# Older value rows copied on the chip by GpSimd instead of loaded, and small constants loaded from ScalarE's queue

## The chip, the cores and the metric

The kernel runs on one core of a Trainium2 chip. The metric is the device time of one execution in microseconds, as a median of runs. Engines are named as in the profile: PE (TensorE, matmuls; PEld its weight loads), DVE (VectorE), ACT (ScalarE), POOL (GpSimd), SP (SyncE, which here only issues DMAs). A DMA can be issued from the queue of any engine that has one; here nearly all are issued by SP, some indirect ones by POOL.

## The reference: what is computed

Attention with a local window and a few global keys, then a mixture of experts with one expert per token.

```python
# attention: B=4, H=8, S=768, D=64, n_global=8, n_local=96
scores = scale * q @ k.T - slope[h] * dist
keep = (key < n_global) | ((0 <= row - key) & (row - key < n_local))
a = softmax(where(keep, scores, -1e9)) ; attn = a @ v
# experts: x = attn as (3072, 512), E=8, F=1024
logits = x @ w_gate + modality_bias[modality_id]
e = argmax(logits) ; g = softmax(logits)[e]
out = g * (relu(x @ w1[e]) @ w2[e])
```

All is fp32. So a block of 128 queries needs the values of its own 128 tokens, of the 96 tokens ahead of it, and of the first 8 tokens of its batch.

## The kernel before

**Blocks and steps.** The 3072 tokens are 24 blocks of 128 (6 per batch). `step(n)`, n from 0 to 24, writes out by hand what PE, ACT and DVE do, in order (a manual schedule): scores of block n (`s_mm`, L257), their reduction and exponential (`red`: DVE L276, ACT L287), the values' product of block n-2 (`pv`), transposes of the probabilities of block n-1 (`t_mm` on PE L301, `t_cp` on DVE L310), normalisation and store of block n-2 (`xr`, L355 and L362), parts of the gate of blocks n-3 and n-4, transposes of the queries and keys of block n+1 (`k_mm` L215, `k_cp` with ACT L228 and DVE L224, L233), the copies of values `copyv(n-1)` on POOL, and whatever is due in that step (`todo`: constants, routing, planning, the first expert's weights). The order on SP and POOL is not by hand: a scheduler sets it, from a list of what each instruction waits for.

**Values.** Scores of a block are two halves of 64 queries, and `pv` multiplies, for each half, a 40-row part (L322) and a 128-row part (L334). There are four kinds of tiles. `va[r]` (four of them) holds a block's 128 value rows for all heads, loaded by SP (L122, 256 KB). `vo` (three) is the 128-row operand of the first half: 64 rows of this block (POOL copy L135) and the upper 64 rows of the block before (POOL copy L137). `vl[r]` (four) is the 40-row operand: for each half, in partitions 0 to 31 for even heads and 64 to 95 for odd ones, 32 older value rows, and in partitions 32 to 39 and 96 to 103 the 8 global rows, which POOL copies from `vg` (L142) when a buffer is first used in a batch. The 32 older rows are rows 32 to 63 of the block before for the first half and rows 64 to 95 for the second. `loadv` loads them from HBM with four DMAs of 32 KB for every block that isn't the first of its batch. `loadv(1)` is called twice, once ahead of the steps (L1048) and again in step 0, so block 1's values are loaded twice.

**Queues.** A DMA counts on one of eight completion semaphores in turn, and its issue waits for the landing of the one eight places before it. SP issues queries, keys and values two to three steps ahead, then stores, zeros for the list of sorted tokens (`consts_c`, L1029, from `zrow`) and weights. `consts_l` (L974 to L981: the gate's weights `wg`, the modality ids `mi`, the modality bias `mb`, the two sizes `gi`) is due in step 1 and is issued by SP. ACT starts with the table load that belongs to L228.

**Routing.** When a batch of blocks has been gated, `route_a` and `route_b` work out every token's position in its expert's list; for the first three batches POOL does this (L427 to L433: `base`, `pos`). `route_d` on DVE takes them up (L442, L444), and `route_c` on POOL scatters the token numbers, two scatters of 128 tokens a step (L450). The copies on POOL that come after such a pair in its order carry waits for its landing. Steps 18 to 20 scatter the second batch; then SP loads the first units' token lists (`uie`), POOL gathers their rows (`xge`, L628), and the third batch's positions follow. After step 24 the experts begin: the first layer of the units in `eslots`, then the rest.

Of the kernel before, what the change touches and what calls it, by code (L numbers as in the profile page):

```python
# [12 lines left out]
I32 = mybir.dt.int32  # L13
# [6 lines left out]
P = 128  # L20
B, H, S, D = 4, 8, 768, 64
NP = H // 2
DM = H * D
E = 8
FF = 1024
NT = B * S
NBLK = NT // P
# [40 lines left out]
def moe_attention_kernel(ctx, tc, q, k, v, n_global, n_local, modality, w_gate, mod_bias, w1, w2, out):  # L68
    nc = tc.nc
# [39 lines left out]
    NV = 4  # L109
    va = [a1.tile([P, H, D], F32, name=f"va{i}") for i in range(NV)]  # L110
    vo = [a1.tile([P, H, D], F32, name=f"vo{i}") for i in range(3)]
    vl = [a1.tile([P, 2, NP, D], F32, name=f"vl{i}") for i in range(NV)]
# [4 lines left out]
    def loadv(n):  # L117
        b, i = n // NB, n % NB
        r, a = n % NV, P * i

        def rows(dst, r0, cnt, hs):
            nc.sync.dma_start(dst, v[b, hs, r0 : r0 + cnt, :].rearrange("h s d -> s h d"))  # L122

        rows(va[r], a, P, slice(0, H))
        if i == 0:
            for h in range(2):
                rows(vg[b % 2][64 * h + 32 : 64 * h + C1], 0, NG0, slice(h, H, 2))
        else:
            for x in range(2):
                for h in range(2):  # L130
                    rows(vl[r][64 * h : 64 * h + 32, x], a - 96 + 64 * x, 32, slice(h, H, 2))

    def copyv(n):
        b, i, r = n // NB, n % NB, n % NV
        nc.gpsimd.tensor_copy(vo[n % 3][0:64], va[r][0:64])  # L135
        if i:
            nc.gpsimd.tensor_copy(vo[n % 3][64:P], va[(n - 1) % NV][64:P])  # L137
        if vb[r] != b:
            vb[r] = b
            for h in range(2):  # L140
                g = slice(64 * h + 32, 64 * h + C1)
                nc.gpsimd.tensor_copy(vl[r][g], vg[b % 2][g].unsqueeze(1).broadcast_to([NG0, 2, NP, D]))  # L142

    load_kq(0)
    load_kq(1)
    loadv(0)


# [534 lines left out]
    def l1_unit(s, f):  # L683
        if f % 2 == 0:
            s.ph = p_t(f"ph{s.name}{f}")
        fs = slice(f * P, (f + 1) * P)
        o = s.ph[:, f % 2 * U : (f % 2 + 1) * U]
        for c in range(4):
            hi, lo = s.hi["a", c], s.lo["a", c]
            nc.tensor.matmul(o, hi[:, fs], s.xh[:, c, :], start=(c == 0), stop=False)  # L690
            nc.tensor.matmul(o, hi[:, fs], s.xl[:, c, :], start=False, stop=False)  # L691
            nc.tensor.matmul(o, lo[:, fs], s.xh[:, c, :], start=False, stop=(c == 3))  # L692
        if f % 2:
            fsl = slice(f - 1, f + 1)
            pv = s.ph.rearrange("p (f n) -> p f n", f=2)
            nc.scalar.activation(s.hh[:, fsl, :], pv, AF.Relu)  # L696
            V.scalar_tensor_tensor(s.hl[:, fsl, :], pv, 0.0, s.hh[:, fsl, :].bitcast(F32), ALU.max, ALU.subtract)  # L697
# [227 lines left out]
    def at(n, f, *args):  # L925
        todo.setdefault(n, []).append((f, args))
# [5 lines left out]
    wg = const.tile([P, 4, 32], F32, name="wg")  # L932
# [38 lines left out]
    mod = {}  # L971

    def consts_l():
        nc.sync.dma_start(wg[:, :, 0:E], w_gate.rearrange("(c p) e -> p c e", p=P))  # L974
        mi = gp.tile([NBLK, P, 2], I32, tag="mi", name="mi", bufs=1)
        nc.sync.dma_start(mi, modality.bitcast(I32).rearrange("(t p w) -> t p w", t=NBLK, w=2))
        mb = gp.tile([P, 2, E], F32, tag="mb", name="mb", bufs=1)
        nc.sync.dma_start(mb, mod_bias.rearrange("(o m) e -> o m e", o=1).broadcast_to([P, 2, E]))
        gi = gp.tile([P, 2, 2], I32, tag="gi", name="gi", bufs=1)
        for j, src in enumerate((n_global, n_local)):  # L980
            nc.sync.dma_start(  # L981
                gi[:, j, :], src.bitcast(I32).rearrange("(o w) -> o w", o=1).broadcast_to([P, 2])
            )
        mod["mi"], mod["mb"], mod["gi"] = mi, mb, gi
# [47 lines left out]
    for b in range(B):  # L1032
# [4 lines left out]
        for j in range(NB):  # L1037
            at(n0 + NB + (6 + j // 2 if b + 1 < B else 5), route_c, b, j)
    at(1, consts_a)
    at(1, consts_l)  # L1040
    at(3, consts_b)
    for j in range(8):
        at(3 + j, consts_c, j)
    at(4, consts_d)
    for h in range(H):
        table(tbl, h, mm)
    load_kq(2)
    loadv(1)  # L1048

    early = {}  # L1050
# [46 lines left out]
    def l1_first(f):  # L1097
        l1_unit(eslots[0], f)

    man_pe = tc.manual_schedule(engines={ET.PE})  # L1100
    man_pe.__enter__()
    man = tc.manual_schedule(engines={ET.Activation, ET.DVE})
# [2 lines left out]
    def load(n):  # L1105

        if n + 3 < NBLK:
            load_kq(n + 3)
        if n + LV < NBLK:
            loadv(n + LV)  # L1110
# [10 lines left out]
    def step(n):  # L1121
# [36 lines left out]
        if back:  # L1158
            t_mm(n - 1, 3)
            t_cp(n - 1, 3, not on)  # L1160
            copyv(n - 1)
# [103 lines left out]
    for u in range(nslot):  # L1265
# [3 lines left out]
        for m in range(0 if u else LF, 16):  # L1269
            if m >= 8:  # L1270
                for t in range(s.halves):
                    if u + 1 < nslot or s.halves == 1:
                        l2(s, m - 8, t)
                    else:
                        p = 2 * (m - 8) + t
# [102 lines left out]
```

## Time and profile before

| | us |
|---|---|
| median of 3 runs | 502.28 (501.94 to 502.31) |
| the profiled execution's own time | 504.03 |
| its span in the trace | 502.2 |
| granted TensorE clock, mean | 0.987 |
| attention, to about | 190 |
| experts, from about | 190 |

The trace is of the profiled execution, so its durations belong to 504.03 us, not to the median. In its rows a start time is followed by the busy time, the engine, the line, the operation, what it writes and reads, and in brackets how long the engine had waited and for whom. SPq is SP's queue, with the time that the issue of a DMA took. In rows of stretches stand the busy time of PE, PEld, DVE, ACT and POOL, then the granted clock, the busy share of the DMA engines and the GB/s that they moved.

### The profile page before, as it was taken

The numbers are of one execution on the slowest core, as the hardware profiler recorded it, in microseconds if no ns is written. First come the engines' busy times: TensorE is split into PE (matmuls) and PEld (weight loads), VectorE is DVE, ScalarE is ACT, GpSimd is POOL, SyncE is SP. The second block draws the span as 40 slices with busy tenths as digits, with TensorE's granted clock in tenths as the row PEclk, the third lists the DMA queues.
The fourth block names the chain that finished last, engine by engine and source line by source line (L and its number), as shares of the span: only waits on it lengthen the run. The fifth ranks groups of instructions, "written<-read, shape, count | busy, mean of one in ns | idle before, by whom it ended". The sixth has DMA issues, their size and how long they took to land.

```text
span 502.2 us, 15068 instructions
## 1 busy us (share of the span) xinstructions
PE 468.6 (93%) x5789; PEld 419.4 (84%) x5789; DVE 343.1 (68%) x999; ACT 297.5 (59%) x716; POOL 156.3 (31%) x234
## 2 busy tenths in 40 slices
PE   7879899999898989999999999899999999999991
PEld 6778899999787869898989898798988998798980
DVE  5868788978987874997756477474765748556530
ACT  6747777777667763546456466464665557555420
POOL 9513314545443355062130405204041040500100
PEclk9989999999989999999999999999999999999997
DMA  9778878787668934767785849778598666965100
GB/s 175 152 215 206 200 168 215 180 196 192 158 160 248 287 128 150 265 188 246 232 277 199 275 154 325 246 220 292 159 332 269 205 248 218 321 225 165 44 22 26
DMA packets 125509, 102.75 MB, mean 205 GB/s; under 512 B 96283, under 2 KB 97715, under 8 KB 125428
## 3 DMA queue, kind: packets, MB, share of 16 engines
q1 hardware_dynamic: 120660, 88.65, 60.8%
q0 software_dynamic: 4768, 13.05, 7.2%
q8 instruction: 47, 0.77, 0.6%
q14 instruction: 34, 0.28, 0.2%
HBM read 87.31 MB, written 14.63 MB: 203 GB/s over the span
## 4 chain that ended last, share of the span: by engine, by line
PE 44%; issue 12%; DVE 2%; DMA 2%; POOL 1%; ACT 0%; SPq 0%; POOLq 0%; DVEq 0%; ACTq 0%
PE phs L692 5%; PE phs L690 4%; PE phs L691 4%; PE pos L730 4%; PE pos L729 4%; PE pos L728 4%; PE phe L690 2%; PE phe L691 2%; PE phe L692 2%; PE poe L728 2%; PE poe L730 2%; PE poe L729 2%; DMA uig<-ids_sorted 2%; POOL out L744 1%; PE mts L673 1%
## 5 line engine op out<-in xcount | busy, mean ns | idle before, releaser
L287 ACT ACTIVATE pr<-sc,nmx 128x168 f32<-128x168 f32 x192 | 81.1, 423 | 30.5 <-DVE nmx L276 29.4
L692 PE MATMUL phs<-xhs,als 128*128 128x256 f32 x256 | 72.5, 283 | 0.6 <-DVE als L662 0.5
L690 PE MATMUL phs<-xhs,ahs 128*128 128x256 f32 x256 | 72.2, 282 | 0.0
L691 PE MATMUL phs<-xls,ahs 128*128 128x256 f32 x256 | 72.1, 282 | 0.0
L628 POOL DMA_INDIRECT xgs<-x_rows,uis x16 | 27.1, 1694 | 131.5 <-DMA uis<-ids_sorted 66.9
L276 DVE CUSTOM_DVE_ANT_0 sc<-s,tbl 128x168 f32<-128x168 f32 x192 | 52.1, 327 | 9.4 <-PE s L257 9.4
L697 DVE SCALAR_TENSOR_TENSOR hls<-phs,hhs 128x512 fp32r<-128x512 f32 x32 | 22.1, 692 | 51.0 <-ACT hhs L696 51.0
L301 PE MATMUL pt<-ident,pr 128*128 128x128 f32 x288 | 47.2, 288 | 7.3 <-DVE pT L310 4.7
L728 PE MATMUL pos<-bhs,hhs 128*128 128x512 f32 x128 | 51.4, 401 | 0.0
L730 PE MATMUL pos<-bhs,hls 128*128 128x512 f32 x128 | 50.6, 395 | 0.0
L729 PE MATMUL pos<-bls,hhs 128*128 128x512 f32 x128 | 50.5, 395 | 0.0
L692 PEld LDWEIGHTS phs<-xhs,als 128*128 128x128 f32 x256 | 48.8, 191 | 1.0 <-DVE als L662 1.0
L310 DVE COPY pT<-pt 128x384 f32<-128x384 f32 x71 | 38.9, 548 | 15.5 <-PE pt L301 15.4
L690 PEld LDWEIGHTS phs<-xhs,ahs 128*128 128x128 f32 x256 | 48.9, 191 | 0.4
L691 PEld LDWEIGHTS phs<-xls,ahs 128*128 128x128 f32 x256 | 48.8, 191 | 0.3
L696 ACT ACTIVATE hhs<-phs 128x512 fp32r<-128x512 f32 x32 | 19.1, 597 | 50.0 <-PE phs L692 50.0
L257 PEld LDWEIGHTS s<-kt,qt 64*64 64x64 f32 x1536 | 38.2, 132 | 10.4 <-ACT kt L228 6.1
L257 PE MATMUL s<-kt,qt 64*64 64x128 f32 (+1 forms) x1536 | 41.7, 248 | 4.7 <-ACT kt L228 1.8
L301 PEld LDWEIGHTS pt<-ident,pr 128*128 128x128 f32 x288 | 32.4, 144 | 13.1 <-DVE pT L310 5.4
L450 POOL DMA_INDIRECT ids_sorted<-tki,pi x24 | 25.4, 1060 | 34.7 <-DVE remb L508 17.6
L287 ACT ACTIVATION_READ_ACCUMULATOR pr<-sc,nmx 128x1 f32 x192 | 35.9, 187 | 0.0
L744 POOL DMA_INDIRECT out<-obs,ois x16 | 17.1, 1069 | 47.7 <-ACT obs L743 44.6
(343 smaller groups left out, 1251.2 us busy)
## 6 DMA issues: line engine op xcount, KB each, us to landing
va<-in_v SPq DMA_DIRECT2D x25, 256.0 KB, 4.2
kn<-in_k SPq DMA_DIRECT2D x24, 256.0 KB, 4.0
qn<-in_q SPq DMA_DIRECT2D x24, 256.0 KB, 5.0
x_rows<-xr SPq DMA_DIRECT2D x24, 256.0 KB, 3.7
vl<-in_v SPq DMA_DIRECT2D x84, 32.0 KB, 3.0
rawe0a<-in_moe_w SPq DMA_DIRECT2D x4, 512.0 KB, 5.9
rawe0b<-in_moe_w SPq DMA_DIRECT2D x4, 512.0 KB
rawe1a<-in_moe_w SPq DMA_DIRECT2D x4, 512.0 KB, 3.5
```

Source lines behind the costliest of these rows:

```text
L257: nc.tensor.matmul(ps[h][64 * half : 64 * half + 64, c : c + cnt], qt[hs, hp, 64 * half : 64 * half + 64], keys, start=True, stop=True,)
L276: V.tensor_tensor_reduce(out=sc, in0=pss[n, hp // 2][h][:, hp % 2 * W : (hp % 2 + 1) * W], in1=(tbl0 if n % NB == 0 else tbl)[:, hh, :], o ...
L287: last[0] = nc.scalar.activation(pr[:, h * (PRW - W) : h * (PRW - W) + W], sc, AF.Exp, bias=nmx[:, hh : hh + 1], scale=-1.0, accum_out=sum ...
L301: nc.tensor.transpose(tp[:, j * P : (j + 1) * P], pr[:, o : o + P], ident)
L310: V.tensor_copy(pT.rearrange("p a b -> p (a b)"), tp[:, 0 : 3 * P])
L628: nc.gpsimd.indirect_dma_start(out=s.xg[:, t, :], out_offset=None, in_=s.xsrc, in_offset=bass.IndirectOffsetOnAxis(ap=s.ui[:, t, 0:1], axi ...
L690: nc.tensor.matmul(o, hi[:, fs], s.xh[:, c, :], start=(c == 0), stop=False)
L691: nc.tensor.matmul(o, hi[:, fs], s.xl[:, c, :], start=False, stop=False)
L692: nc.tensor.matmul(o, lo[:, fs], s.xh[:, c, :], start=False, stop=(c == 3))
L728: nc.tensor.matmul(s.po[t], s.hh[:, fc, tt], hi[:, wv], start=(fc == 0), stop=False)
L729: nc.tensor.matmul(s.po[t], s.hh[:, fc, tt], lo[:, wv], start=False, stop=False)
L730: nc.tensor.matmul(s.po[t], s.hl[:, fc, tt], hi[:, wv], start=False, stop=(fc == 7))
```

## The change

Two things. `loadv` no longer loads the older 32 rows; `copyv` copies them on POOL from the `va` tile of the block before, four copies of 32 partitions x 256 columns for each block with a predecessor (new L138), each to other partitions than it reads from. That is 80 copies for 84 DMAs of 32 KB. And `consts_l` issues its five DMAs from ACT's queue, and is called ahead of the manual schedules instead of in step 1. What PE and DVE do, and in which order, is unchanged. Lines of the changed kernel are shifted: L135, L137 and L142 become L131, L134 and L143, and later ones are one higher.

```diff
--- before.py
+++ after.py
@@ -125,16 +125,17 @@
         if i == 0:
             for h in range(2):
                 rows(vg[b % 2][64 * h + 32 : 64 * h + C1], 0, NG0, slice(h, H, 2))
-        else:
-            for x in range(2):
-                for h in range(2):
-                    rows(vl[r][64 * h : 64 * h + 32, x], a - 96 + 64 * x, 32, slice(h, H, 2))
 
     def copyv(n):
         b, i, r = n // NB, n % NB, n % NV
         nc.gpsimd.tensor_copy(vo[n % 3][0:64], va[r][0:64])
         if i:
-            nc.gpsimd.tensor_copy(vo[n % 3][64:P], va[(n - 1) % NV][64:P])
+            back = va[(n - 1) % NV]
+            nc.gpsimd.tensor_copy(vo[n % 3][64:P], back[64:P])
+
+            for x in range(2):
+                for h in range(2):
+                    nc.gpsimd.tensor_copy(vl[r][64 * h : 64 * h + 32, x], back[64 * x + 32 : 64 * x + 64, h:H:2])
         if vb[r] != b:
             vb[r] = b
             for h in range(2):
@@ -971,14 +972,14 @@
     mod = {}
 
     def consts_l():
-        nc.sync.dma_start(wg[:, :, 0:E], w_gate.rearrange("(c p) e -> p c e", p=P))
+        nc.scalar.dma_start(wg[:, :, 0:E], w_gate.rearrange("(c p) e -> p c e", p=P))
         mi = gp.tile([NBLK, P, 2], I32, tag="mi", name="mi", bufs=1)
-        nc.sync.dma_start(mi, modality.bitcast(I32).rearrange("(t p w) -> t p w", t=NBLK, w=2))
+        nc.scalar.dma_start(mi, modality.bitcast(I32).rearrange("(t p w) -> t p w", t=NBLK, w=2))
         mb = gp.tile([P, 2, E], F32, tag="mb", name="mb", bufs=1)
-        nc.sync.dma_start(mb, mod_bias.rearrange("(o m) e -> o m e", o=1).broadcast_to([P, 2, E]))
+        nc.scalar.dma_start(mb, mod_bias.rearrange("(o m) e -> o m e", o=1).broadcast_to([P, 2, E]))
         gi = gp.tile([P, 2, 2], I32, tag="gi", name="gi", bufs=1)
         for j, src in enumerate((n_global, n_local)):
-            nc.sync.dma_start(
+            nc.scalar.dma_start(
                 gi[:, j, :], src.bitcast(I32).rearrange("(o w) -> o w", o=1).broadcast_to([P, 2])
             )
         mod["mi"], mod["mb"], mod["gi"] = mi, mb, gi
@@ -1037,7 +1038,6 @@
         for j in range(NB):
             at(n0 + NB + (6 + j // 2 if b + 1 < B else 5), route_c, b, j)
     at(1, consts_a)
-    at(1, consts_l)
     at(3, consts_b)
     for j in range(8):
         at(3 + j, consts_c, j)
@@ -1097,6 +1097,7 @@
     def l1_first(f):
         l1_unit(eslots[0], f)
 
+    consts_l()
     man_pe = tc.manual_schedule(engines={ET.PE})
     man_pe.__enter__()
     man = tc.manual_schedule(engines={ET.Activation, ET.DVE})
```

SP's order in the fill, before, from block 3's keys to the second load of block 1's values (`kn`, `qn`: keys and queries; `va_76` to `va_79` are the four `va`, `vl_83` to `vl_86` the four `vl`):

```order
L105 DMA kn_274<-in_k 128x8x64
L105 DMA qn_275<-in_q 128x8x64
L122 DMA va_78<-in_v 128x8x64
L122 DMA vl_85<-in_v 32x4x64 x4
L974 DMA wg<-in_moe_w_gate 128x4x8
L105 DMA kn_358<-in_k 128x8x64
L105 DMA qn_359<-in_q 128x8x64
L976 DMA mi<-in_moe_modality_id 24x256
L978 DMA mb<-in_moe_modality_bias 128x16
L981 DMA gi<-in_n_global 128x2
L122 DMA va_77<-in_v 128x8x64
L122 DMA vl_84<-in_v 32x4x64 x4
```

and the same stretch now (`ids_sorted<-zrow` are the zeros of `consts_c`):

```order
L105 DMA kn_278<-in_k 128x8x64
L105 DMA qn_279<-in_q 128x8x64
L122 DMA va_78<-in_v 128x8x64
L122 DMA va_79<-in_v 128x8x64
L1030 DMA ids_sorted<-zrow 128x388 x2
L122 DMA vg_88<-in_v 8x4x64 x2
L105 DMA kn_358<-in_k 128x8x64
L105 DMA qn_359<-in_q 128x8x64
L1030 DMA ids_sorted<-zrow 128x388 x4
L122 DMA va_77<-in_v 128x8x64
L1030 DMA ids_sorted<-zrow 128x388 x2
```

The loads of `vl` and of the constants are gone from it, and block 3's values and six writes of zeros have moved ahead of the second load of `va_77`.

On ACT the five constants now stand ahead of its first table load (L228, now L229): `mi`, `mb`, `gi` twice, then `wg`, which waits for an earlier DMA's landing and for POOL's memset of `wg` (L970). All else on ACT keeps its order.

POOL's order from the second scatter of step 20 to the third batch's positions (`base`), before (waits on DMASW are for the landing of scatters and gathers):

```order
L450 DMA ids_sorted<-tki,pi_3287 24832x16
L628 DMA xge_4275<-x_rows,uie_4064 128x512 [waits DMAHW4_49,DMAHW3_49,DMAHW7_49,DMAHW1_49,DVE_49]
L628 DMA xge_4275<-x_rows,uie_4064 128x512
L628 DMA xge_4278<-x_rows,uie_4075 128x512 [waits DMAHW5_49]
L628 DMA xge_4278<-x_rows,uie_4075 128x512
L135 COPY vo_81<-va_78 64x512 [waits DMAHW1_49,PE_49]
L137 COPY vo_81<-va_77 64x512 [waits DMASW5_49,DMASW6_49,DMASW4_49,DMASW7_49,DMASW3_49,DMASW2_49]
L135 COPY vo_82<-va_79 64x512 [waits DMAHW5_49,PE_49]
L137 COPY vo_82<-va_78 64x512
L427 TENSOR_TENSOR base<-base,pks_4262 128x8 [waits DVE_49,Pool_49]
```

and now:

```order
L451 DMA ids_sorted<-tki,pi_3279 24832x16
L138 COPY vl_86<-va_78 32x256 [waits DMASW3_49,DMAHW2_49,DMASW2_49,PE_49]
L138 COPY vl_86<-va_78 32x256 [waits PE_49] x3
L131 COPY vo_81<-va_78 64x512 [waits PE_49,Pool_49]
L134 COPY vo_81<-va_77 64x512 [waits Pool_49]
L629 DMA xge_4263<-x_rows,uie_4052 128x512 [waits DMAHW3_49,DMAHW4_49,DMAHW1_49,DMAHW7_49,DVE_49,Pool_49]
L629 DMA xge_4263<-x_rows,uie_4052 128x512
L629 DMA xge_4266<-x_rows,uie_4063 128x512 [waits DMAHW5_49]
L629 DMA xge_4266<-x_rows,uie_4063 128x512
L131 COPY vo_82<-va_79 64x512 [waits DMAHW7_49,PE_49]
L134 COPY vo_82<-va_78 64x512 [waits DMASW6_49,DMASW7_49,DMASW5_49,DMASW4_49]
L428 TENSOR_TENSOR base<-base,pks_4250 128x8 [waits DVE_49,Pool_49]
```

The four copies of `vl_86`, the first with a wait for that step's scatters, and the two of `vo_81` now stand ahead of the gathers. Behind the scatters of steps 18 and 19 it is the same: four copies of a `vl`, the first waiting for the landing, then the two copies of a `vo`, of which the first did not have that wait before.

## The prediction

> **What bounds the kernel now.** I read the page first, then busy time by stretches, then PE's timeline where the stretches show a hole. On the page, PE is the busiest engine:
>
> ```profile
> PE 468.6 (93%) x5789; PEld 419.4 (84%) x5789; DVE 343.1 (68%) x999; ACT 297.5 (59%) x716; POOL 156.3 (31%) x234
> ```
>
> The stretches (PE, PEld, DVE, ACT, POOL busy; granted clock; DMA share; GB/s) say where the other 7% lies:
>
> ```profile
> 20.00:30.00 10.00, 7.47 (x169) 6.51 (x165) 6.62 (x34) 6.79 (x30) 2.66 (x5) 0.94 0.62 144
> 30.00:40.00 10.00, 9.23 (x178) 8.50 (x177) 8.00 (x36) 5.46 (x21) 0.00 (x0) 0.89 0.79 229
> 60.00:70.00 10.00, 10.00 (x207) 9.31 (x207) 7.65 (x32) 7.22 (x27) 1.21 (x2) 1.00 0.73 176
> 130.00:140.00 10.00, 7.61 (x161) 6.76 (x160) 9.03 (x41) 5.15 (x20) 2.88 (x5) 0.90 0.68 167
> 180.00:190.00 10.00, 8.37 (x145) 7.52 (x142) 7.42 (x19) 5.06 (x9) 4.83 (x9) 1.00 0.39 129
> 260.00:280.00 20.00, 20.00 (x137) 18.41 (x136) 10.53 (x13) 10.17 (x14) 3.17 (x3) 1.00 0.64 216
> ```
>
> The expert stage (260:280) is PE without a gap, and so is attention in its middle (60:70). A change in attention's loads can move the end only where PE has holes: the fill up to 40 us, the routing burst near 135 us, the hand-over near 183 us.
>
> **The early stall, term B.** PE's rows at step 3 of attention (begins at 23.81, the next step at 35.15), and the rows of POOL and of SP's queue that belong to them:
>
> ```profile
> 23.81 1.61 PE L257 MATMUL s<-kt,qt 64*64 64x128 f32 x64 [0.35 <-ACT kt L228]
> 26.16 0.30 PE L322 MATMUL x<-vl,pT 40*64 40x64 f32 x2 [0.75 <-DMA vl<-in_v]
> 27.57 0.85 PE L322 MATMUL x<-vl,pT 40*64 40x64 f32 x30 [1.11 <-DMA vl<-in_v]
> 35.15 1.10 PE L257 MATMUL s<-kt,qt 64*64 64x128 f32 x37
> ```
>
> ```profile
> 25.90 0.60 POOL L135 COPY vo<-va 64x512 f32<-64x512 f32 x1 [5.67 <-DMA va<-in_v]
> ```
>
> ```profile
> 21.54 0.43 SPq L122 DMA_DIRECT2D va<-in_v  x1
> 22.02 2.15 SPq L122 DMA_DIRECT2D vl<-in_v  x4
> ```
>
> PE waits 0.75 + 1.11 = 1.86 us for the second load of block 1's vl and va (block 1 is loaded twice). The clock then drops: 0.94 in 20:30 and 0.89 in 30:40 are 0.6 + 1.1 = 1.7 us of lost clock. Step 3 takes 35.15 - 23.81 = 11.3 us. After the change vl comes from POOL, and only va's second load can stall PE. When does it land? By the order on SP it is the 15th load of 256 KB, behind six writes of 128x388 words (0.2 MB each). Rates from two stretches:
>
> ```profile
> 2.00:10.00 8.00, 6.37 (x112) 6.11 (x111) 4.56 (x24) 3.85 (x18) 7.67 (x39) 1.00 1.18 227
> 34.00:36.00 2.00, 1.37 (x46) 1.14 (x50) 1.56 (x7) 0.41 (x2) 0.00 (x0) 1.00 1.09 353
> ```
>
> 15 x 0.262 MB at 227 GB/s is 17.3 us, 1.2 MB at 353 GB/s (a stretch of such writes) 3.4 us; from 2 us on that ends near 22.7, and landing takes a little longer: 24 us as an estimate. PE would begin L322 at 26.16 - 0.75 = 25.4 and needs POOL's copy of va 0.85 later, at 26.3; landing at 24 plus 0.6 of copying makes it. So both the wait and the slow clock go: B = -3.6. If va lands 2 us later than that, SP having to wait for its own completions, nothing is gained (0); if only the idle time shrinks and the slow window stays, -1.9.
>
> **ACT's start, term A.** Five DMA issues now stand ahead of ACT's table load, the last of them (wg) waiting for GpSimd's memset of wg:
>
> ```profile
> 0.79 1.28 ACT L228 ACT_TABLE_LOAD   x1 [0.79 <-PEq L1363]
> 5.71 0.58 ACT L228 COPY kt<-tr 128x512 f32<-128x512 f32 x1 [3.64 <-PE tr L215]
> ```
>
> ```profile
> 4.18 0.21 POOL L970 MEMSET wg<- 128x128 f32 x1
> 17.49 0.38 SPq L974 DMA_DIRECT2D wg<-in_moe_w_gate  x1
> 6.55 0.45 DVE L233 COPY kt<-kt 128x96 f32<-128x96 f32 x1
> ```
>
> Four issues fit into the first 4 us. The fifth starts at 4.39, takes 0.38, the table load 1.28: the kt copy starts at 6.1 instead of 5.71. DVE takes kt at 6.55, 0.26 after the copy's end at 6.29, so some 0.1 to 0.2 reach PE. A = +0.3, from 0 to 1.3 (a whole table load). The constants' absence from SP frees some 2 us of issue; that is in B.
>
> **POOL's 80 copies.** Their price is not in the trace; the nearest are
>
> ```profile
> L135 POOL COPY vo<-va x24: 602/604/608, 13.0 to 177.3; 64x512 f32<-64x512 f32 x24
> 130.73 0.45 POOL L233 COPY kt<-kt 128x320 f32<-128x320 f32 x1 [1.66 <-ACT kt L228]
> ```
>
> 320 columns 0.45, 512 columns 0.60: 256 columns are 0.40, with a start-to-start distance of 0.44; no less than half of 0.60 and no more than 0.60. Four per block are 1.76 us (1.2 to 2.4). In the middle of attention POOL is busy 1.21 of 10 us, and a block's values are used by PE a step after its copies, so 1.76 per step of some 6.5 us is hidden: 0. If that cover were gone, PE would wait 1.76 a step. The 80 loads that go were hidden as well after step 3: PE is full while DMA stands at 0.73.
>
> **The routing burst, term C.** At 131 to 135 us DVE has a row of small operations, and PE waits for DVE behind it:
>
> ```profile
> 132.31 0.17 DVE L482 TENSOR_SCALAR cie<-cie 128x8 int32<-128x8 int32 x1
> 133.44 0.55 DVE L492 TENSOR_SCALAR first_used<-cexe 128x8 f32<-128x8 f32 x1
> 134.70 0.62 DVE L494 TENSOR_TENSOR first_used<-first_used,fulle 128x8 f32<-128x8 f32 x1
> ```
>
> ```profile
> 133.36 1.28 POOL L142 COPY vl<-vg 8x512 f32<-8x512 f32 x2 [2.18 <-PE x L322]
> ```
>
> ```profile
> 135.97 0.63 PE L369 MATMUL tx<-ident,xr 128*128 128x128 f32 x4 [1.11 <-DVE nmx L276]
> 137.88 0.88 PE L301 MATMUL pt<-ident,pr 128*128 128x128 f32 x3 [1.29 <-DVE pT L310]
> ```
>
> The same kind of operation takes 0.17 with POOL idle and 0.55 to 0.62 while POOL copies. POOL's queue now reaches this place later and fuller, so up to eight more such operations (L439 to L489) can be held, 0.4 each: 3.2 at most, 0 if POOL's copies fall elsewhere. I take +1.0: two or three held, the nearest case being the three held now. The Trainium skill (GPSIMD Engine Reference, 1. Specifications) says that GpSimd shares its SBUF interfaces with VectorE, with contention for two-port modes or two SBUF inputs; by the second condition alone only L485 and L489 of these would be held, C = +0.8 and the sum 503.1. The trace has L492, with one input, held too.
>
> **The hand-over, term D.** POOL's rows of the last scatters, the gathers and the third positions, and who waits:
>
> ```profile
> 146.29 1.27 POOL L142 COPY vl<-vg 8x512 f32<-8x512 f32 x2 [2.13 <-DMA ids_sorted<-tki,pi]
> 149.50 0.98 POOL L450 DMA_INDIRECT ids_sorted<-tki,pi  x1 [0.61 <-ACT lps L380]
> 152.03 0.60 POOL L135 COPY vo<-va 64x512 f32<-64x512 f32 x1 [0.28 <-PE x L334]
> 156.65 0.61 POOL L137 COPY vo<-va 64x512 f32<-64x512 f32 x1 [4.01 <-DMA ids_sorted<-tki,pi]
> 157.54 0.98 POOL L450 DMA_INDIRECT ids_sorted<-tki,pi  x1 [0.28 <-POOL vo L137]
> 165.16 1.00 POOL L628 DMA_INDIRECT xge<-x_rows,uie  x1 [5.39 <-DVE oh L409]
> 176.65 0.61 POOL L137 COPY vo<-va 64x512 f32<-64x512 f32 x1 [5.88 <-DMA xge<-x_rows,uie]
> 178.66 1.59 POOL L427 TENSOR_TENSOR base<-base,pks 128x8 f32<-128x8 f32 x6
> ```
>
> ```profile
> 181.26 0.20 DVE L442 TENSOR_REDUCE pf<-pos 128x6 f32<-128x48 f32 x1 [1.71 <-POOL pos L433]
> ```
>
> ```profile
> 183.68 0.88 PE L301 MATMUL pt<-ident,pr 128*128 128x128 f32 x6 [1.63 <-DVE pT L310]
> ```
>
> POOL's positions already hold DVE (1.71) and through it PE (1.63), so a later POOL costs its full delay. The copies of vl wait for the scatters' landing, and what follows them waits with them. First landing: 1.76 more, less the 0.61 that the scatter waited anyway: second scatter +1.15. Second landing: 1.76 for vl, 0.65 for the vo copy that no longer lies under the wait: third scatter +3.6. Its landing releases the loads of the gathers' indices, and also vl and two vo copies (3.06 us): the first gather +3.9. Behind the gathers' landing stands one vo copy where there were three: 1.3 comes back. D = +2.5; with 0.3 per copy instead of 0.44 and one landing shorter +0.5, with 0.6 per copy +4.
>
> PE's hole there grows to 1.63 + 2.5 = 4.1 us, longer than the 1.86 that the slow clock followed at 28 us. Such a drop costs up to 1.7 (B's number), and less where PE waits for the first weights anyway: W = +0.8, from 0 to 1.7.
>
> **Sum.** -3.6 + 0.3 + 1.0 + 2.5 + 0.8 = +1.0. The profiled execution took 504.03 us (span 502.2), the median of the runs is 502.28; on the former the change makes 505.0, on the latter 503.3, which I give. This kernel can be measured to about 0.2%, 1.0 us.
>
> **Rivals.**
> - *The tail does not pay* (faster). PE's steps set when the scatters start; with vl's loads gone the landings (2.13, 4.01, 5.88 us) may shorten by as much as POOL lost, since those 4 us waits share the DMA with loads of 256-byte packets. Then D and W vanish: -3.6 + 0.3 + 1.0 = -2.3, 500.0; with C = 0, 499.0. It decides once the landings shorten by 2.5 in all. For it: the chain is mostly waiting for DMA. Against it: the DMA share is 0.39 there, little to be freed. Chance 0.30.
> - *Slow clock moves to the tail* (slower). Short pieces of idle time are not what slowed the clock at 28 us, and the window stays; a 4.1 us hole is enough for one: -1.9 + 0.3 + 1.0 + 2.5 + 1.7 = +3.6, 505.9. The Trainium skill (TensorE: Matmul & The Clock Gate, Part 1) lets the clock fall to half after at least one idle window of about 3.4 us, which is this case. The trace speaks against its first half: 1.86 us of waits in two pieces came just before the drop. The same sum comes out if va's load is merely half late. Chance 0.14.
> - *Nothing arrives* (no change): the early gain meets another wait of the fill, POOL's delay sits under PE's waits: 502.3. Against it: PE shows no other wait over 0.8 us at step 3. Chance 0.10.
> - *The forecast*, 503.3, own range 501.5 to 504.8: chance 0.46.
>
> **How the numbers follow.** Slower by over 0.2%: 0.27 of the forecast's 0.46, 0.13 of the slow clock's 0.14, 0.02 of the last: 0.42. Within 0.2%: 0.16 + 0.04 (tail partly paid) + 0.01 + 0.07 = 0.28. Faster: 0.26 + 0.03 + 0.01 = 0.30. The range goes from 499.5, between the tail-free cases, to 505.9, the slow clock's case.
>
> **What would show it.** B: no wait of PE at L322 in step 3, clock 1.00 in 20:40, step 3 near 7.7 us. A: kt's first copy at 6.1. Copies of vl at 0.40. C: more small DVE operations over 0.4 in the burst. D: DVE waiting 4 us for POOL's positions, and PE as long. Wrong if va's second load lands after 26 us, or if DVE's wait for the positions stays under 2.5 us.

## The result and the profile after

The changed kernel takes 508.08 us (median of 5 runs, 507.08 to 514.17) where the kernel before takes 502.31 in the same comparison (501.94 to 504.25): a ratio of 1.0124, 95% interval 1.0074 to 1.0173. It is slower by 5.8 us. The forecast was 503.3, +1.0, with a range to 505.9: the sign was right, the size far too small, and the measured time lies outside the range.

The profiled execution is the slowest of the five, 514.17 us (span 512.4) against 504.03 before: 10.1 us. I read it first by landmarks. The table gives when DVE's first score reduction of a step starts, and PE's first expert matmul and last matmul (us):

| | before | after | difference |
|---|---|---|---|
| step 2 | 18.99 | 22.86 | +3.9 |
| step 4 | 36.41 | 38.49 | +2.1 |
| step 13 | 98.38 | 101.72 | +3.3 |
| step 18 | 135.24 | 140.16 | +4.9 |
| step 23 | 173.96 | 176.43 | +2.5 |
| first expert matmul | 188.33 | 198.75 | +10.4 |
| last matmul | 490.72 | 501.21 | +10.5 |

The experts cost nothing. Almost 8 us arise between step 23 and the first expert matmul and 4 us up to step 2; between these the two traces drift by +1.6 to -2.4 us from landmark to landmark. The stretches that answer to these places (columns as in the prediction; the last line is of the kernel before):

```profile
0.00:10.00 10.00, 5.80 (x53) 5.19 (x57) 3.52 (x18) 4.13 (x14) 8.72 (x45) 0.90 0.66 141
10.00:20.00 10.00, 8.29 (x153) 7.58 (x148) 5.94 (x36) 6.88 (x30) 9.14 (x19) 0.75 1.08 228
...
60.00:70.00 10.00, 8.30 (x170) 7.95 (x171) 5.43 (x26) 5.19 (x21) 3.91 (x9) 0.83 0.47 112
...
180.00:190.00 10.00, 4.05 (x87) 3.38 (x87) 3.60 (x13) 3.17 (x8) 2.70 (x11) 0.95 0.53 197
190.00:200.00 10.00, 9.60 (x102) 8.63 (x103) 5.60 (x14) 4.39 (x7) 5.74 (x6) 0.54 0.42 137
200.00:210.00 10.00, 10.00 (x93) 9.30 (x92) 3.66 (x13) 2.26 (x6) 2.50 (x3) 1.00 0.38 133
```

```profile
190.00:200.00 10.00, 10.00 (x93) 9.30 (x92) 3.59 (x14) 2.80 (x7) 5.40 (x5) 1.00 0.48 143
```

In 180:190 PE works 4 of 10 us. In 190:200 it is busy, but its clock is 0.54, so it does little: before, the same stretch held the full-speed work that here comes at 200:210 (93 matmuls in both).

**The hand-over.** POOL's rows, then DVE's and PE's:

```profile
146.07 1.03 POOL L451 DMA_INDIRECT ids_sorted<-tki,pi  x1 [3.87 <-issue]
...
155.24 0.98 POOL L451 DMA_INDIRECT ids_sorted<-tki,pi  x1 [0.28 <-POOL vo L134]
156.53 0.95 POOL L451 DMA_INDIRECT ids_sorted<-tki,pi  x1 [0.30 <-issue]
162.18 1.74 POOL L138 COPY vl<-va 32x256 f32<-32x256 f32 x4 [4.69 <-DMA va<-in_v]
163.98 0.61 POOL L131 COPY vo<-va 64x512 f32<-64x512 f32 x1
164.64 0.61 POOL L134 COPY vo<-va 64x512 f32<-64x512 f32 x1
165.53 0.98 POOL L451 DMA_INDIRECT ids_sorted<-tki,pi  x1 [0.28 <-POOL vo L134]
...
173.36 1.01 POOL L629 DMA_INDIRECT xge<-x_rows,uie  x1 [1.18 <-DVE xr L356]
...
184.68 0.61 POOL L134 COPY vo<-va 64x512 f32<-64x512 f32 x1 [5.47 <-DMA xge<-x_rows,uie]
185.38 1.59 POOL L428 TENSOR_TENSOR base<-base,pks 128x8 f32<-128x8 f32 x6
```

```profile
187.97 0.20 DVE L443 TENSOR_REDUCE pf<-pos 128x6 f32<-128x48 f32 x1 [5.96 <-POOL pos L434]
```

```profile
190.40 1.54 PE L302 MATMUL pt<-ident,pr 128*128 128x128 f32 x6 [5.87 <-DVE pT L311]
...
198.75 0.56 PE L691 MATMUL phe<-xhe,ahe 128*128 128x256 f32 x1
```

and PE's first expert matmul before:

```profile
188.33 0.36 PE L690 MATMUL phe<-xhe,ahe 128*128 128x256 f32 x1
```

Behind a scatter's landing POOL now does four copies of vl and two of vo before the next scatter. (For the copies at 162.18 the profile names a load of va as what ended the wait; by POOL's order they wait for the scatters too, and they begin 4.70 us after the scatter's end, as the copy behind the same scatters did before, 4.90.) DVE waits 5.96 us for the positions (1.71 before), PE 5.87 (1.63). The six transposes at 190.40 take 1.54 where they took 0.88: the clock is at half from 189.0 to 199.2.

**The start.** PE's first transposes and scores and the issue on SP beside them, with the row of before's issue last:

```profile
5.00 0.61 PE L216 MATMUL tr<-ident,kn 128*128 128x128 f32 x4
7.89 0.97 PE L216 MATMUL tr<-ident,qn 128*128 128x128 f32 x4 [2.28 <-DMA qn<-in_q]
9.74 2.85 PE L258 MATMUL s<-kt,qt 64*64 64x128 f32 x64 [0.88 <-DVE qt L225]
```

```profile
4.36 3.25 SPq L122 DMA_DIRECT2D va<-in_v  x1
```

```profile
4.13 0.88 SPq L122 DMA_DIRECT2D va<-in_v  x1
```

PE waits 2.28 us for the first queries, and the scores run at half clock. ACT's own start is as forecast: its table load is at 4.86 and kt's copy at 6.16.

The experiments below came in five sets of runs, each with the kernel before in it: in the first four PE was held back between 100 and 200 us in every kernel (medians of 524 to 537 us, before among them), in the fifth before took 504, and a ratio leaves out the runs more than 1.5% above its own kernel's fastest. So times are compared only within a set, and the traces of the first four are read mostly up to step 13, where the steps run as above.

### The profile page after: what moved, and what is told of

It is laid out like the page before. It is cut to its first block, busy times and chain, and to the rows that moved or that the text cites. A ratio compares the mean times of both kernels' runs of the same rounds, so it can differ in the third digit from the quotient of the medians.

```text
span 512.4 us, 15019 instructions
## 1 busy us (share of the span) xinstructions
PE 473.3 (92%) x5789; PEld 423.0 (83%) x5789; DVE 343.4 (67%) x999; ACT 297.7 (58%) x716; POOL 188.9 (37%) x314
## 4 chain that ended last, share of the span: by engine, by line
PE 39%; issue 13%; DVE 4%; DMA 4%; POOL 1%; ACT 1%; SPq 1%; POOLq 0%; DVEq 0%
PE phs L693 4%; PE phs L691 4%; PE phs L692 4%; DMA uig<-ids_sorted 4%; PE pos L731 3%; PE pos L730 3%; PE pos L729 3%; PE phe L691 2%; PE phe L692 2%; PE phe L693 2%; PE poe L729 2%; PE poe L731 2%; PE poe L730 2%; DVE blg L663 1%; DVE alg L663 1%
## 5 line engine op out<-in xcount | busy, mean ns | idle before, releaser
L629 POOL DMA_INDIRECT xgs<-x_rows,uis x16 | 29.9, 1869 | 130.0 <-DMA uis<-ids_sorted 65.4
L277 DVE CUSTOM_DVE_ANT_0 sc<-s,tbl 128x168 f32<-128x168 f32 x192 | 52.1, 326 | 10.3 <-PE s L258 10.3
L258 PEld LDWEIGHTS s<-kt,qt 64*64 64x64 f32 x1536 | 39.4, 136 | 9.8 <-ACT kt L229 4.8
L138 POOL COPY vl<-va 32x256 f32<-32x256 f32 x80 | 31.5, 394 | 39.5 <-PE x L323 16.8
L302 PEld LDWEIGHTS pt<-ident,pr 128*128 128x128 f32 x288 | 32.3, 144 | 15.8 <-DVE pT L311 10.3
```

Of the source, the lines that this page charges most:

```text
L138: nc.gpsimd.tensor_copy(vl[r][64 * h : 64 * h + 32, x], back[64 * x + 32 : 64 * x + 64, h:H:2])
L258: nc.tensor.matmul(ps[h][64 * half : 64 * half + 64, c : c + cnt], qt[hs, hp, 64 * half : 64 * half + 64], keys, start=True, stop=True,)
L277: V.tensor_tensor_reduce(out=sc, in0=pss[n, hp // 2][h][:, hp % 2 * W : (hp % 2 + 1) * W], in1=(tbl0 if n % NB == 0 else tbl)[:, hh, :], o ...
L302: nc.tensor.transpose(tp[:, j * P : (j + 1) * P], pr[:, o : o + P], ident)
```

## The experiments

Ratios are to the kernel before in the same set, with 95% intervals; the last column is the ratio of the medians of all runs:

| kernel | set | ratio | of medians |
|---|---|---|---|
| whole change, again | 1 | 1.0055 (0.9994 to 1.0115) | 0.9973 |
| | 4 | 1.0107 (1.0035 to 1.0179) | 1.0083 |
| copies alone | 1 | 1.0089 (1.0039 to 1.0138) | 1.0016 |
| | 2 | 1.0028 (0.9940 to 1.0117) | 1.0062 |
| | 3 | 0.9974 (0.9930 to 1.0019) | 0.9979 |
| constants alone | 1 | 1.0040 (0.9955 to 1.0126) | 1.0011 |
| | 2 | 0.9970 (0.9882 to 1.0058) | 0.9992 |
| | 3 | 1.0023 (0.9936 to 1.0110) | 1.0022 |
| tail undone, constants on SP | 1 | 1.0162 (1.0072 to 1.0251) | 1.0081 |
| tail undone alone | 3 | 1.0140 (1.0073 to 1.0207) | 1.0050 |
| | 4 | 1.0114 (1.0009 to 1.0219) | 1.0111 |
| | 5 | 0.9993 (0.9960 to 1.0026) | 0.9986 |
| positions on DVE | 2 | 1.0042 (1.0007 to 1.0078) | 1.0051 |
| tail undone, one load of block 1, constants on SP | 2 | 1.0006 (0.9958 to 1.0054) | 1.0004 |
| | 3 | 1.0110 (1.0052 to 1.0168) | 0.9996 |
| | 4 | 1.0124 (1.0022 to 1.0227) | 1.0112 |
| before itself | 5 | 0.9988 (0.9951 to 1.0025) | 0.9996 |

In the first four sets the ratio of one kernel differs by up to 1.2% between sets, and the two columns by up to 1.1%, so these tell little; the traces and the fifth set tell more. The whole change itself was not run in the fifth set.

**The tail alone undone.** From block 17 on the older rows are loaded as before; POOL's order in the last steps is then that of before.

```diff
+        elif n >= 17:
+            for x in range(2):
+                for h in range(2):
+                    rows(vl[r][64 * h : 64 * h + 32, x], a - 96 + 64 * x, 32, slice(h, H, 2))
...
-            for x in range(2):
+            for x in range(2 if n < 17 else 0):
                 for h in range(2):
                     nc.gpsimd.tensor_copy(vl[r][64 * h : 64 * h + 32, x], back[64 * x + 32 : 64 * x + 64, h:H:2])
```

> The whole change with the older rows of blocks 17 and later loaded as before, against before. Theory: where PE runs steadily, DVE's wait for the positions is under 2 us, no slow window follows the hand-over, and the time is within 1.5 of before, where the whole change was 5.8 over it; where PE is slowed, that wait is hidden in all kernels and the time is within 1 % of before. Rival: over before by 4 or more with PE steady, so that the loss lies elsewhere than in the tail.

It took 503.68 us (500.56 to 507.44, 12 runs) beside 504.41 of before (501.34 to 508.90, 23 runs): 0.9993 (0.9960 to 1.0026), where the whole change had 1.0124 (1.0074 to 1.0173) against its own before. DVE's wait and PE's hole, and the stretch after:

```profile
182.61 0.20 DVE L447 TENSOR_REDUCE pf<-pos 128x6 f32<-128x48 f32 x1 [1.39 <-POOL pos L438]
```

```profile
185.04 0.88 PE L306 MATMUL pt<-ident,pr 128*128 128x128 f32 x6 [1.31 <-DVE pT L315]
...
189.69 0.36 PE L695 MATMUL phe<-xhe,ahe 128*128 128x256 f32 x1
```

```profile
190.00:200.00 10.00, 10.00 (x93) 9.30 (x93) 4.89 (x17) 2.84 (x7) 6.46 (x6) 1.00 0.56 185
```

The wait is 1.39, the hole 1.31, the clock stays at 1.00, and from the hole's end to the first expert matmul PE takes 4.65 us as in before (188.33 - 183.68), where the whole change took 8.35 (198.75 - 190.40). So the loss lies in the last blocks' copies, as far as two comparisons of different sets can say it: the two intervals lie apart, and the long wait, the long hole and the slow clock are gone from the trace. The two earlier runs of this kernel, and the variant with the constants on SP, had expected the same:

> The whole change, but the older rows of blocks 17 and later are loaded as before; POOL's order in the last steps is then that of before. This undoes the tail alone. Theory (the copies hold POOL's chain of scatters, gathers and positions): where PE runs steadily, DVE's wait for the positions falls from 6 to under 2 us and the time is 5 to 8 below the whole change. Where PE is slowed between 100 and 200 us, the chain is hidden and the time is that of the whole change within 3. Rival: the wait stays over 4 us, since the gathers' landing sets it and not the copies.

> The whole change with the older rows of blocks 17 and later loaded as before (the tail alone undone). Theory: on a chip that runs PE steadily DVE's wait for the positions is under 2 us, no slow window follows, and the time is 5 to 8 below the whole change, about 1 below before. Rival: the gathers' own landing sets the wait, 4 us or more, and the time is that of the whole change.

> The copies for blocks up to 16 only; from block 17 on the older rows are loaded as before, and the constants are issued by SP in step 1. Theory (the scatters' landing holds the copies and these hold the positions): the hole of PE at the hand-over is back at 1.6, and the early gain is kept, so 498.5 to 501.5, below before. Rival: the copies cost by POOL's load everywhere (holding DVE, or buffers coming free later): between before and the copies alone, 503 to 505, the hole still over 3.

In the first four sets DVE does not wait for the third batch's positions in any kernel but the one with triple copies below, as PE and DVE come to them later, so undoing the tail could not help and did not (1.0114 to 1.0162). The last, with a forecast of 498.5 to 501.5, missed also because its early gain was not there: its step 4 begins at 37.80, against 36.41.

**Before itself**, for its trace in the fifth set:

> The kernel before itself, for its trace in the state of these chips. Theory: up to step 13 its steps are those of the trace shown, with PE waiting for vl and va in step 3, and step 4 begins 1 us later than in the whole change; from 100 us on PE is slowed as in the other kernels, DVE does not wait for the positions, and the last part is as long as theirs. Rival: before is not slowed there, so that the slowing belongs to the change.

It took 504.23 us and was not held back, so the theory failed. Nor does the holding back belong to the change, as the rival has it, since the kernel with the tail undone was not held back in this set either. Step 4 begins at 35.25, no later than in the whole change (35.50 and 35.40 below) and 1.2 us sooner than in the trace of the prediction (36.41): PE has the same two waits for vl, somewhat shorter, but no slow clock after them, as the two stretches show.

```profile
26.37 0.66 PE L322 MATMUL x<-vl,pT 40*64 40x64 f32 x6 [0.47 <-DMA vl<-in_v]
28.02 0.68 PE L322 MATMUL x<-vl,pT 40*64 40x64 f32 x26 [0.99 <-DMA vl<-in_v]
```

```profile
20.00:30.00 10.00, 7.58 (x179) 6.58 (x175) 6.83 (x38) 7.29 (x32) 2.98 (x6) 1.00 0.60 138
30.00:40.00 10.00, 9.19 (x187) 8.33 (x185) 8.97 (x38) 6.69 (x25) 0.20 (x1) 1.00 0.71 203
```

So the slow clock of step 3, half of the gain that the prediction counted on, comes in some executions and not in others. In a trace of the constants alone, whose loads of values are those of before, the two waits are as long as in the prediction's trace (0.77 and 1.09 us), and the clock stays at 1.00.

**The copies of blocks 17 and later made three times**, with the same result:

```diff
+                    for again in range(3 if n >= 17 else 1):
+                        nc.gpsimd.tensor_copy(vl[r][64 * h : 64 * h + 32, x], back[64 * x + 32 : 64 * x + 64, h:H:2])
-                    nc.gpsimd.tensor_copy(vl[r][64 * h : 64 * h + 32, x], back[64 * x + 32 : 64 * x + 64, h:H:2])
```

> The whole change with each copy of the older rows made three times for blocks 17 and later, with the same result: 3.5 us more on POOL behind each landing. It makes the chain visible also where PE is slowed. Theory (POOL's copies behind the scatters' landings set when the positions are ready): POOL's chain from the first scatter of step 18 to the positions is 8 to 11 us longer than with single copies, and DVE waits for the positions 6 to 10 us where PE is slowed, 14 to 17 where it isn't; a slow clock follows. Rival (the landings set it, and copies lie beside them): the chain is within 3 us of the single one, and DVE does not wait more.

544.0 us in one execution, beside 523.7 of before and 528.1 of the whole change in the same set. DVE waits for the positions twice:

```profile
149.47 0.20 DVE L444 TENSOR_REDUCE pf<-pos 128x6 f32<-128x48 f32 x1 [12.62 <-POOL pos L435]
```

```profile
208.76 0.20 DVE L444 TENSOR_REDUCE pf<-pos 128x6 f32<-128x48 f32 x1 [5.14 <-POOL pos L435]
```

The first is for the second batch's positions, where the scheduler has put copies between POOL's steps; the second is the place of the prediction, and shorter than the 6 to 10 us expected. The chain from the first scatter of step 18 to the positions is 51.0 us against 46.4 for the whole change in the same set: +4.6, between the theory's 8 to 11 and the rival's 3. In the whole change of that set POOL itself waits in this chain for PE and DVE (4.05 us for a vo buffer, 2.66 for `pks`), and the longer copies can use up such waits first. What the run shows is that more copying on POOL comes back as DVE's wait for POOL's positions; what one copy costs there it does not show.

**The whole change again**

> The changed kernel once more, for its spread: its profiled execution took 514.17 us where the median of five runs is 508.08. If the losses at the start (late qn, slow clock) and at the hand-over (DVE waiting for POOL's positions) are set by the program, both stand in this profile again: second load of qn0 not ahead of 7 us, a hole of PE of 5 to 6 us at the hand-over, and a time of 507 to 509. If the slow start belongs to that one execution, its rows are missing here and the time is the same.

> The whole change once more beside it. Theory: where PE runs steadily, 5 to 6 over before, most of it in DVE's 6 us wait for POOL's positions and the slow clock after it; at step 4 it is 1 us ahead of before. Where PE is slowed, the wait is hidden and the time is that of before.

The late start belongs to one execution: here the first score begins at 7.91 and 7.74 (9.74 in the profile after). DVE does not wait for the third batch's positions in either. The second was expected to take the time of before where that wait is hidden, and has 1.0107; but in that set every kernel, tail undone or not, has a ratio of 1.01, so this does not tell them apart. Step 4 begins at 35.50 and 35.40. In step 3 PE waits, now for POOL's vo copy, which waits for va's second load. From the second of them, SP's queue, POOL and PE:

```profile
19.07 2.93 SPq L1030 DMA_DIRECT2D ids_sorted<-zrow  x4
22.04 0.47 SPq L122 DMA_DIRECT2D va<-in_v  x1
```

```profile
25.94 0.60 POOL L131 COPY vo<-va 64x512 f32<-64x512 f32 x1 [1.74 <-DMA va<-in_v]
```

```profile
26.60 0.27 PE L335 MATMUL x<-vo,pT 128*64 128x64 f32 x1 [0.71 <-POOL vo L131]
```

SP issues the load at 22.04, where it was issued at 21.54 before, and it lands 3.9 us later. In the fifth set's kernel with the tail undone it was issued at 23.29, and PE waited longer:

```profile
30.07 0.27 PE L339 MATMUL x<-vo,pT 128*64 128x64 f32 x1 [3.80 <-POOL vo L135]
```

**The copies alone** (constants issued by SP in step 1):

> The copies alone: the constants are issued by SP in step 1, as before. Theory: the constants cost the start (PE's first query transposes at 7.9 instead of 5.5, then a slow clock), the copies cost the hand-over. Then the first score starts again near 7.75, the hole at the hand-over stays at 4 us or more, and the time is 503 to 506, 2 to 4 below the whole change. Rival: the copies cost all of it, by POOL being full in the first 30 us, and the constants nothing: 507 to 509.

> The copies alone, the constants issued by SP in step 1 as before, on another chip if there is one that does not stall PE as the first did. Theory: without the constants on ACT the first score starts at 7.75 (with them 7.9 to 9.7); va's second load lands late, so PE waits some 2 us for POOL's vo copy in step 3; the hole at the hand-over is 4 to 6 us. Time 1 to 6 over before. Rival: the constants made the loss and the copies alone are within 1 of before.

> The copies alone, constants on SP in step 1. Theory: a hole of 4 to 6 us at the hand-over where PE runs steadily, PE waiting about 2 us in step 3 for va's second load, first score at 7.5 to 7.8: 2 to 6 over before. Rival (the constants are the loss): within 1 of before.

First scores at 7.52 to 7.76, as in before. In step 3 PE waits 2.1 us for POOL's vo copy in each of the three, and step 4 begins at 36.42 to 37.59, a microsecond or more after the 35.5 and 35.4 of the whole change above: SP issues the constants ahead of va's second load. DVE does not wait for the positions in these sets, so they do not show the price of the hand-over.

**The constants alone**

> The kernel before with only the constants moved to ACT's queue at the start. Theory: qn0 lands 2 us later, a slow window may follow, and the time is 1 to 4 above before (503.5 to 506.5); the early stall at vl and va stays or shrinks a little. Rival (the prediction's term A): only the table load comes 0.4 later, within 0.5 of before.

> The constants alone. Theory: the first score starts 0.2 to 2 later, nothing else changes, the hole at the hand-over is 1.6: 0 to 2 over before. Rival (constants are the loss): 4 or more over before.

> The constants alone. Theory: first score 0.2 to 0.5 later, up to 2 in some executions, waits of step 3 as before: within 0.5 to 2 over before. Rival: 4 or more over before.

No loss that could be measured; all three intervals hold 1. First scores begin at 8.25, 7.95 and 7.72. But SP's fifth load (va) takes 2.0 to 3.1 us to issue in these three, 1.8 to 3.3 in the eight other traces with the constants on ACT, and 0.9 to 1.5 in the nine without. The late start of the profile after, with 3.25, goes with it, but one such issue (3.25 again, in the fifth set's kernel with the tail undone) had no late start behind it.

**Positions of the third batch on DVE** (`eng = nc.gpsimd if b + 2 < B else V`):

> The whole change, but the third batch's positions are worked out by DVE and not by POOL, so that nothing of DVE or PE waits for POOL's queue at the hand-over. Theory: PE's hole there goes from 5.9 to under 1.5 and no slow window follows; against some 2 us more of DVE work in step 22, the time falls by 3 to 6 below the whole change, to 502 to 505. Rival: the hole is that of the gathers or of the first weights and stays; the time is that of the whole change or 1 to 2 more.

1.0042 (1.0007 to 1.0078) in the second set, where the wait is not there to be removed; it does not tell the theories apart.

**Tail undone, block 1 loaded once, constants on SP**

```diff
     load_kq(2)
-    loadv(1)
```

> Copies for blocks up to 16, loads from block 17 on (POOL's order in the last steps is then that of before), the constants on SP in step 1, and block 1's values loaded once. Theory: neither the stall of step 3 (no second load to wait for) nor the longer hole at the hand-over: 2 to 4 below before, 498 to 500.5. Rival: losses come from POOL's use all along attention: at or above before, with waits for POOL or held DVE operations between 40 and 130 us.

> Copies for blocks up to 16, loads from block 17, block 1's values loaded once, constants on SP in step 1. On two other chips its step 4 began 1.4 us sooner than any other kernel's, without a wait in step 3. Theory: 2 to 4 below before where PE runs steadily. Rival: the gain of the fill is given back by the hand-over, within 1 of before.

> Copies for blocks up to 16, loads from block 17, block 1's values loaded once, constants on SP in step 1. Theory: at step 4 it is 2.5 ahead of before, and the hand-over is that of before: 2 to 4 below before where PE runs steadily. Rival: within 1 of before, given back later.

No wait for values in step 3, and step 4 begins at 33.67, 34.04 and 33.27, about 1 us or more ahead of every trace with another kernel (35.02 and later). The ratios range from 1.0006 to 1.0124 in the second to fourth sets, so a gain at the end is not shown.

## Why the prediction was wrong, step by step

- **What bounds the kernel**: right in that the experts did not change and that the two large differences lie in the fill and at the hand-over. The middle of attention differs too, by waits of PE that no engine or DMA of the program ends (1.84 us at 61.70 with a slow clock after it, 1.32 at 111.52); they are treated in the last section.
- **Price of a copy**: right. 0.40 forecast; the group in the profile after has a mean of 394 ns:

```profile
L138 POOL COPY vl<-va 32x256 f32<-32x256 f32 x80 | 31.5, 394 | 39.5 <-PE x L323 16.8
```

- **Term A** (+0.3): right for ACT (table load at 4.86, kt's copy 0.45 later), incomplete for the queues. It counted the constants' issues and not their packets: SP's loads are held up in the first 8 us, and the first score comes 0 to 0.6 us later in ten of the eleven traces with the constants on ACT; in the profiled one it comes 2 us later, and step 2, with the slow clock, 3.9.
- **Term B** (-3.6): failed. The step that failed is the landing of va's second load, "15 x 0.262 MB at 227 GB/s ... 24 us as an estimate". It took the bytes ahead of the load and a rate, and not SP's queue: with the whole change's early part SP issues the load at 22.0 to 23.3 us, no sooner than before (21.5 and 21.9), although the loads of vl and the constants are gone from its order. The four writes ahead of it take 2.93 us to issue, some 0.7 each, where a single issue takes 0.4 to 0.5; which earlier landings they wait for the trace does not show. The load then lands 3.9 to 6.1 us after its issue, at 25.9 to 29.4 us (landing after 26 was the prediction's own sign of being wrong), and PE waits 0.5 to 3.8 us for POOL's vo copy in place of vl. The lower bound named there (0) is what came: step 4 begins at 35.1 to 39.1 with the whole change's early part, at 35.3 and 36.4 in the two traces of before. In the profile after itself PE does not wait for this load, as it is 4 us late from the start. The wait goes when block 1 is loaded once.
- **Term C** (+1.0): too large. At the burst PE waits 1.18 and 1.43, against 1.11 and 1.29: +0.2. One more small operation is held (L440, 0.60 us), not two or three. Beside POOL's copies of vl at 137.84 to 138.66 DVE's small operations take 0.17 to 0.32, where the same ones took 0.17 to 0.23 before, so not every copy on POOL holds them, as the term assumed.

```profile
140.89 0.63 PE L370 MATMUL tx<-ident,xr 128*128 128x128 f32 x4 [1.18 <-DVE nmx L277]
142.95 0.55 PE L302 MATMUL pt<-ident,pr 128*128 128x128 f32 x3 [1.43 <-DVE pT L311]
```

- **Term D** (+2.5): the chain was right at each link. Counted from the first scatter (141.86 before, 146.07 after): second scatter +1.5 (forecast +1.15), third +3.8 (+3.6), first gather +4.0 (+3.9), positions' first step +2.5 (+2.5). PE's hole grew by 4.2, not 2.5, as PE came to it 1.7 us sooner after the first scatter: before, PE lost 1.74 at 160.64 in a wait that the profile after does not have there.

```profile
160.64 0.55 PE L301 MATMUL pt<-ident,pr 128*128 128x128 f32 x3 [1.74 <-issue]
```

  The two traces of the fifth set wait at the same transposes (1.47 with the tail undone, 3.56 before), so whether this wait's absence belongs to the change or to that one execution is open. In the total it cancels: what PE does not lose there it loses in the hole.
- **Term W** (+0.8, at most 1.7): the mis-sized term. The slow clock lasts 10.2 us, three times the one of step 3, and costs 3.7 us (8.35 against 4.65 from the hole's end to the first expert matmul). The Trainium skill (TensorE: Matmul & The Clock Gate, Part 1) has the clock fall to half after at least one idle window of about 3.4 us, and the trace agrees for this hole of 5.87; that it stays low for 10.2 us is this trace's own figure. The fall after 1.84 us, in the last section, does not fit that window. The 10.2 us are a long case: behind 16 holes of 3.5 to 6.3 us in the first four sets the clock stayed at half for 3.4 us (three) or 6.8 (thirteen).
- **Sum**: with B at about -0.5 (an estimate from where step 4 begins), A and C at +0.2 each, D at +2.5 net of the 1.7 above, and W at +3.7, it is +6.1, and the median rose by 5.8. Of the 5.1 between this and the forecast +1.0, B makes 3.1 and W 2.9, and C takes 0.8 off. The terms come from single traces, so the agreement of the sum with the median is in part luck. That undoing the tail brings the ratio from 1.0124 to 0.9993 says that the rest is about even. The right sign was owed to D and W; it came with a gain in the fill that was not there. The rival "slow clock moves to the tail" named the place and the mechanism, with less than half of the clock's price in this trace.

What stays open: how much of the 5.8 is the hole and how much the clock, execution by execution; only one execution of the whole change that was not held back between 100 and 200 us was profiled, and it is the slowest of five.

## What to carry to other kernels

Work that is moved to an idle engine is not free where that engine has a chain of its own: look where in its strict order the new work stands behind a wait, and add the whole delay where another engine already waits for that chain's end. A hole of several microseconds in PE costs more than its length, so price the slow clock after it by the longest that could follow (here 3.4 to 10.2 us at half speed), not by the shortest seen. And a load's landing is not its bytes over a rate: ask first when its queue gets to issue it.

## What the runs showed of the hardware

- After PE's hole of 5.87 us the clock was at half for 10.2 us; after a wait of 1.84 us at 61.70 for 3.4: over 62 to 67 the clock's mean is 0.66, which is 1.7 us lost, or 3.4 at half; over 189 to 200 it is 0.53, 5.2 lost, some 10.3 at half. In all twenty traces, up to 250 us, each such stay is 3.4 us or two, three or four times that. Whether the clock falls is not settled by the length of a short wait alone: in step 3 it did not fall after waits of 1.46 us in all (before, fifth set), 1.86 (constants alone) or 2.08 and 2.15 (copies alone), and it did after 1.86 (before, the prediction's trace) and 2.11 (copies alone).

```profile
62.00:67.00 5.00, 5.00 (x43) 4.91 (x43) 2.86 (x8) 1.85 (x5) 1.54 (x3) 0.66 0.41 111
189.00:200.00 11.00, 9.60 (x102) 8.63 (x103) 6.56 (x17) 4.39 (x7) 5.74 (x6) 0.53 0.39 124
```

- In attention PE loses 1.0 to 3.6 us at a time in waits that no engine or DMA of the program ends, such as

```profile
61.70 0.22 PE L335 MATMUL x<-vo,pT 128*64 128x64 f32 x1 [1.84 <-issue]
```

  There are three over a microsecond in attention in the profile after, two in the one before, and two (2.53 and 3.56) in before's trace of the fifth set. They are not spread at random: 13 of the 20 traces have one of 1.4 to 2.0 us at this same matmul. All 19 that last 1.39 us or more (from 25 to 200 us, all traces) end 2.3 to 2.8 us after a packet of the DMA queue that the profile calls "instruction" (31 packets in the first 200 us of the profile after). The loading of instructions is thus a likely cause, but no run tried it. A slow clock can follow; these waits are part of the spread between runs.

```profile
q8 instruction: 47, 0.77, 0.6%
```

- With 996 packets and 0.05 MB of constants on a second queue SP's issue of one load takes 1.8 to 3.3 us (eleven traces), and 0.9 to 1.5 without them (nine traces):

```profile
q10 hardware_dynamic: 996, 0.05, 0.1%
```
